# Seventeen loads from the sync queue to the GpSimd queue, unit 0 transposed in full-width tiles, and a new table of order, in a fused attention and feed-forward kernel

## The chip, the cores and the metric

The kernel runs on one core of a Trainium2 chip. The metric is device time in microseconds (us), as the median of several runs. Five engines work side by side, each through its own list of instructions in order: TensorE (PE, matrix products and transposes through PSUM), VectorE (DVE), ScalarE (ACT), GpSimd (POOL) and SyncE (SP, which only issues transfers). Transfers (DMAs) run on 16 DMA engines that all issuers share. An engine that waits for a semaphore holds everything behind it in its list.

## The reference

q, k and v have the shape (batch 8, heads 8, sequence 576, head size 64).

```python
def phi(x):
    proj = np.einsum('bhsd,df->bhsf', x, w_phi)             # 64 -> 128 features
    proj = proj - np.max(np.abs(proj), axis=-1, keepdims=True)
    return np.concatenate([np.exp(proj), np.exp(-proj)], axis=-1)
q_p, k_p = phi(q), phi(k)
kv  = np.einsum('bhsf,bhsd->bhfd', k_p, v);  z = np.sum(k_p, axis=2)
att = np.einsum('bhsf,bhfd->bhsd', q_p, kv) / (np.einsum('bhsf,bhf->bhs', q_p, z)[..., None] + 1e-06)
x   = att.transpose(0, 2, 1, 3).reshape(4608, 512)
out = np.maximum(np.maximum(x @ w1, x @ w2), x @ w3) @ w_out   # 512 -> 768 -> 512
```

## The kernel before, in words

**Attention.** There are 16 units of four heads (half a batch each), u0 to u15. A unit's q, k and v come as 128 partitions x 18 tiles of 64 numbers in f32 (576 KB each). q and k are brought to bf16 and turned so that the head size lies on the partitions (tile `qkT`). How this is done differs by unit. For u0 the loads come in halves through SP (line 441), DVE and ACT cast them (L445), and PE transposes (L483). For u1 to u3 the load itself casts; it is issued by POOL (L452), and PE transposes. From u4 on SP loads f32 (L463), POOL casts (L469), and a transposing DMA on SP's queue does the turn (L498). v is always loaded in f32 through SP (L463). In the units that PE transposes, each 128 x 64 block is one half-width transpose, q and k into different halves of the result, and `qk_bf` is laid out as [q or k, tile, 64].

Then PE projects q and k on the features (L525 and L520, tiles `psq`, `psk`), DVE takes the largest magnitude over the features (L544, results `mqp` for q and `mk` for k), ACT takes both exponentials of k (L538, tile `Ek`), and POOL multiplies v by the factors exp(+-mk) (L579, tile `vab`; line 589 adds the column that gives z). For u0 this multiplication may also be placed on DVE (`VA_DVE`, L49 and L582 ff.). The maximum of q is brought in by a second product (L604, or L606 and L609 for u0 and u1; tile `psm`), and ACT takes its exponentials (L617, tile `Eq`). PE forms kv (L633, 72 small products a unit, called K below), then the numerator and denominator (L651, four groups of ten small products a unit, called N; tile `psn`). DVE divides (L657, L658, tile `x_sb`), and x is turned into `xT` by PE (L671, u0 to u3) or by a transposing DMA (L681).

**Feed-forward.** max(max(a, b), c) @ w_out is computed with w2 and w3 replaced by their differences from w1 (L775: six subtractions of a third of a matrix each, called wd), with relu(x(w2-w1)) (L704 `up`, L712/L714), the maximum with x(w3-w1) (L704, L710) and then two parts of the output: hT @ w_out (L737) and x @ (w1 w_out) (L732). The product w1 w_out is formed once: PE transposes w1 (L787, tile `pwT`), ACT and DVE copy it out (L790), PE multiplies (L801). The weights are loaded with a cast by POOL (L413): W0 is w1, W1 and W2 are the other two, W3 is w_out. There are nine chunks of 512 tokens; the last one holds the 64 leftover rows of each batch.

**What sets the order.** No scheduler runs: every piece of work is a node with a number, and a table in the source (`PLAN`) names for each node its engine (T for PE, D for DVE, A for ACT, G for POOL, S for SP), its buffer numbers and a due time. `1081G@5.1` is node 1081 (the load W0) on POOL, due at 5.1. Instructions are emitted in the order of due times (`fill`, L264), so the table fixes each engine's list; the due times are the planner's and bind nothing on the chip. `fill` also puts idle products (L832, `idler`, one 512-column product each) into gaps of PE's due times in the first 28 us. A node's `costs` lists the engines that may take it.

A POOL or SP load whose buffer is not free waits in its queue for the last reader of that buffer. For v of u1 to u3 a one-element copy on DVE (`gate`, L461) is a further condition for the load.

Of the kernel before, what the change touches and what calls it, by code (L numbers as in the profile page):

```python
# [48 lines left out]
VA_DVE = 1  # L49
# [50 lines left out]
56A@14.3 35D@13.4 50A0@14.8 65A@15.0 104T111211@13.5 66T5@13.8 158G2@3.4 68A@15.5 108D@14.0 30D@14.6 46A@15.8 88T6@14.1  # L100
89D@15.2 92T7@14.9 93D@15.8 107D@16.0 60T3@15.3 61A@16.1 94T46@16.0 98D@16.6 105A@16.6 67A@17.1 99T71@16.8 102D@17.2
96A@17.4 62A@17.9 97D@17.9 101A@18.4 157G@4.2 163T5@17.6 164D2@18.5 1081G@5.1 1091T7@18.1 1092D0@19.1 109T34@18.7 112D@20.2
161T0@19.0 1084G@5.9 106A@18.9 110A@19.4 95A@19.9 1095T5@19.6 1096A@20.3 114T2@20.0 117D@20.8 116A@21.3 103D@21.2 162D@21.8
111A@21.7 1093T7@20.4 52G0@15.2 47G@16.3 115A@22.1 53G@17.4 49G@17.7 51G@18.0 48G@19.1 69T063@21.0 71A@22.5 133T51@22.1
134A@22.9 70A@23.4 130T0@22.6 159D2@22.4 113D@22.5 118D@23.1 1094D@23.5 100A@23.8 135A@24.3 230G0@20.2 1082G@21.0 229G@21.8
74T30@23.0 75D0@24.6 1083G@22.7 119A1@24.8 122G1@25.1 132A@25.0 78T4@23.4 127T2@23.7 136T6@24.1 137A@25.5 72T1@24.6
73D1@25.2 79D0@25.8 182T007500@25.0 185D@26.5 184A@26.0 138A@26.5 123A@26.9 186D@27.1 1099T3@25.4 1100D@27.7 1101T1@26.7
1102D@28.3 131A@27.2 129A@27.7 177T46@28.1 87S@7.4 120G@25.4 121G@26.5 172T70@28.3 175D@28.9 76T3@28.6 183A@28.2 128A@28.7
165T5@28.9 166D@29.5 178A@29.1 173A@29.6 179A@30.1 139T1@29.1 174A@30.6 1103T2@29.3 140A@31.1 1104A@31.4 180D@29.7 77D1@30.3
181D@31.0 187T7@30.6 191D@31.6 126G@27.7 125G@27.9 124G@29.1 142T154@30.9 176D@31.9 144A@32.1 141A@32.5 143A@32.9 367S1@17.2  # L110
370G1@30.2 167T36@31.9 171D@32.5 195A0@33.3 169A@33.5 189A@34.0 198A0@34.4 188A@34.5 1085G@31.3 235T2@32.3 236D0@33.1
170D@33.7 82T0@32.9 80T4@33.1 81A@34.9 145T11@33.4 146D0@34.3 147T5@33.8 148D1@35.0 190D@35.6 1097T2@34.1 168A@35.5 83A@36.0
1098A@36.6 149T3@35.4 150D0@35.9 151T1@35.7 152D1@36.5 233T4@36.0 234D@37.2 254T115711@36.6 256A@37.1 237T6@37.0 238D@37.8
257D@38.0 153T3@37.1 192T0@37.4 193A0@37.7 231D3@38.6 154A@37.9 155T2@37.5 156A@38.6 255A@39.2 160S@22.6 197G@33.7
244T14@37.9 247D@38.7 196G@35.8 214T006@38.2 216A@39.7 215D@39.4 245A@40.1 249T35@39.2 250A@40.6 252D@39.8 239T21@39.5
242D@40.4 240A@41.1 251A@41.6 258D@41.0 1090D@41.6 241A@42.1 1107T0@39.9 366S1@27.2 259T6@40.8 263D@42.2 1087G@37.9
1115T3@41.0 1116A1@42.5 1108A@43.0 261A@43.5 246A@43.9 1109T2@41.9 253D@42.5 369G@40.0 1088D@43.1 1117T7@42.7 1118A@44.4
302S0@32.6 305G2@41.1 194S@38.1 199T30@43.6 211T5@43.8 212A@44.9 213A@45.4 200A@45.7 243D@43.8 262D@44.4 248D@44.7
1129T0@43.9 1130D@45.3 1086G@42.2 1111T1@44.8 208T7@45.6 1112D@45.9 1110D@46.5 209A@46.2 267A1@46.7 264T4@45.9 265A1@46.9
1127T5@45.9 1128D@47.1 1113T0@46.8 202T1@47.7 432S1@38.8 435G0@44.3 232S@39.4 268G1@47.1 260A@47.2 210A@47.5 201A@48.0  # L120
1114A@48.5 205T2@47.9 207A@49.0 371S1@41.2 203A@49.5 204A@50.1 1089D@47.8 206A@50.6 372T004600@48.2 376D@48.6 387T57@48.4
389A@51.1 390D@49.2 375D@49.8 1119T3@48.7 1120D@50.4 301S0@44.1 1125T0@49.6 1126D@51.1 373A@51.6 270G@49.2 1121T5@50.5
388A@52.1 377T41@51.4 380D@51.9 1122D@52.5 382T32@51.7 385D@53.1 374A@52.5 1123T0@52.0 1124D@53.7 378A@53.0 1135T4@52.8
219T60@53.7 392T5@54.0 384A@53.5 379A@54.0 394A@54.5 266S@47.3 368S1@48.0 277T31@54.2 278A@54.8 692S0@48.6 431S1@49.3
283T0@54.5 285A@55.3 383A@55.7 304G@49.6 562S1@49.9 306S2@50.8 561S0@55.9 393A@56.2 284A@56.5 1136T@54.6 1137A0@56.8
1138S@57.6 220D0@54.3 381D@54.9 391D@55.5 386D@56.3 217T6@55.9 218D1@56.9 274T1@56.2 275A@57.4 395D@57.5 396D@58.0 276A@58.1
400A0@58.6 279A@58.8 1131T7@56.4 221T0@57.3 222D0@58.4 269G@50.7 286T124@57.7 288D@59.0 280T6@58.8 281A@59.3 223T5@59.0
397T1@59.3 398D0@59.6 287D@59.8 271T0@59.4 273A@59.8 282A@60.3 272A@60.8 402G0@59.0 434G@61.1 564G1@62.2 565G@63.3
225T3@59.6 226D@60.2 224D1@60.6 1132T@59.9 1133A1@61.4 312T114111@61.3 315D@61.7 307T23@61.5 322T65@61.8 323A@62.2 325D@62.3
293T01@62.1 294D0@62.9 310D@63.6 314A@62.7 324A@63.2 313A@63.7 316D@64.3 1139T7@62.4 326D@64.9 227T4@63.3 228D@65.5  # L130
399S@59.9 404T60@63.5 406A@64.1 309A@64.6 405A@65.1 1140T@63.8 327T0@65.1 328A@65.6 563S0@60.6 407T2@65.3 410T1@65.5
412A@65.9 1141A2@66.4 409A@67.0 311D@66.0 330D@66.6 295T5@65.7 411A@67.5 408A@68.0 331D@67.1 296D1@67.4 291T6@66.0
292D0@68.0 1143T4@66.3 289T7@67.2 290D1@68.6 436S0@62.3 303S2@65.2 496S1@65.8 329A@68.5 498S3@66.5 1144T@67.5 1145D3@69.3
308A@68.8 416T1@68.8 418A@69.3 413T5@68.9 415A@69.7 299T2@69.1 300A@70.2 297T6@69.4 298D@69.9 417A@70.8 317T07@69.8
320D@70.4 321D@71.0 695G2@64.4 403G@65.5 401G@65.8 419T034@70.0 421D@71.6 499G0@71.6 332T6@71.2 333D1@72.0 334S@72.3
335A1@71.7 338G1@72.7 337G@73.0 420D@72.2 1155T2@71.2 1167T0@72.1 1156D0@72.6 1168D@73.3 319A@72.0 414A@72.5 318A@73.0
447T001400@73.1 449A@73.5 452T63@73.3 455D@73.9 453A@74.0 437T52@73.5 439A@74.5 448A@75.0 438A@75.5 454A@75.9 440D@74.5
450D@75.1 441D@76.1 1157T7@73.9 1158A@76.4 1165T0@74.7 457T6@75.6 459A@76.9 428T50@75.8 429D0@76.7 566S1@73.0 628S1@75.9
451D@77.3 461D@77.9 1153T1@76.1 1154A@77.3 1166D@78.3 1149T2@77.0 442T75@77.9 443A@78.4 445D@78.9 1150A@78.9 458A@79.4
444A@79.7 336G@75.1 354T114@78.2 356A@80.2 355D@79.5 424T0@79.3 348T21@79.6 349A@80.6 460D@79.9 425D1@80.2 350A@81.2  # L140
# [145 lines left out]
def kernel(  # L286
# [574 lines left out]
```

## Time and profile before

| | |
|---|---|
| runs | 290.39, 292.25 and 293.01 us; median 292.25 |
| span of the profiled execution | 290.5 us, first to last instruction; 1.75 us below the median |
| PE busy | 276.3 us (95%), 3518 products in the records |
| DVE, ACT, POOL busy | 213.8, 193.8, 116.9 us |
| idle products | 23, 8.6 us of PE |
| loads on SP's queue | 16 of v, 12 of k, 12 of q (576 KB each), 4 halves for u0 |
| transfers issued by POOL | 10 (six q or k with a cast, four weights) |

"Busy" counts the time in which an instruction is in the engine. For PE the products overlap, so its busy time also covers products that follow each other at half the pace; the column PEclk gives the clock that PE was granted (1.00 is full). A wait stands with the instruction that it held, and names what released it.

### The profile page before, as it was taken

How to read it: one execution, taken by the hardware profiler on the slowest of the kernel's cores; microseconds unless marked ns; L12 is line 12 of the kernel's file. 1: busy time of each engine (PE TensorE's matmuls, PEld its weight loads, DVE VectorE, ACT ScalarE, POOL GpSimd, SP SyncE). 2: the span in 40 equal slices, each digit the busy share in tenths (PEclk: the TensorE clock that was granted, in tenths of full speed). 3: DMA queues.
4: the chain of work that ended last, by engine and by line, in shares of the span. 5: the costliest groups of instructions: out<-in, count | busy, mean ns of one | idle time of the engine just before them, and what ended most of it. 6: DMA issues, size and time to landing. Idle time of an engine off the chain costs nothing.

```text
span 290.5 us, 8509 instructions
## 1 busy us (share of the span) xinstructions
PE 276.3 (95%) x3518; PEld 157.4 (54%) x3555; DVE 213.8 (74%) x449; ACT 193.8 (67%) x446; POOL 116.9 (40%) x99
## 2 busy tenths in 40 slices
PE   8678999899999999999999999999999999999995
PEld 3447676356656655555555566555544654444443
DVE  5695899998998967988979879878963382455411
ACT  1795989789898989976797898858758510021021
POOL 8055789728373662817180753500077001000000
PEclk9997999999999999999999999999999999999999
DMA  7999967899999999997999545982240109414045
GB/s 184 280 242 199 246 198 181 197 360 212 231 241 361 150 257 253 275 262 157 225 324 273 118 83 156 164 167 45 52 115 2 39 10 208 91 39 95 12 122 170
DMA packets 65649, 50.83 MB, mean 175 GB/s; under 512 B 46154, under 2 KB 50378, under 8 KB 65610
## 3 DMA queue, kind: packets, MB, share of 16 engines
q1 hardware_dynamic: 61279, 45.03, 63.2%
q0 software_dynamic: 4000, 4.92, 9.9%
q8 instruction: 28, 0.46, 0.6%
q10 hardware_dynamic: 331, 0.33, 0.3%
q14 instruction: 11, 0.09, 0.1%
HBM read 34.67 MB, written 9.44 MB: 152 GB/s over the span
## 4 chain that ended last, share of the span: by engine, by line
PE 66%; DMA 13%; DVE 10%; POOL 5%; issue 2%; SPq 2%; ACT 2%; ACTq 0%; POOLq 0%; DVEq 0%
PE ups L704 22%; PE ops L737 13%; PE ops L732 9%; DMA w_bf<-in_moe_w_dram 6%; PE psn L651 5%; DMA qkT<-qk_bf 5%; PE kvps L633 5%; PE psm L604 3%; PE psq L525 3%; DVE mk L544 3%; DVE hT L710 2%; POOL vab L579 2%; DMA q_raw<-in_q_dram 2%; DVE mqp L544 2%; PE pm L801 2%
## 5 line engine op out<-in xcount | busy, mean ns | idle before, releaser
L704 PE MATMUL ups<-xT,w_bf 128*128 128x512 bf16 x412 | 101.7, 379 | 2.5 <-DVE mk L544 0.9
L617 ACT ACTIVATE Eq<-psm 128x512 bf16<-128x512 f32 (+1 forms) x160 | 82.3, 584 | 9.6 <-PE psm L604 8.2
L579 POOL TENSOR_TENSOR vab<-v_raw,em 128x1152 bf16<-128x1152 f32 (+1 forms) x36 | 67.9, 1904 | 44.6 <-ACT em L575 31.7
L538 ACT ACTIVATE Ek<-psk 128x512 bf16<-128x512 f32 x128 | 70.6, 616 | 8.3 <-PE psk L525 5.1
L704 PEld LDWEIGHTS <-w_bf 128*128 128x128 bf16 x432 | 40.6, 98 | 47.2 <-issue 2.3
L544 DVE TENSOR_REDUCE mqp<-psq 128x4 bf16<-128x512 f32 (+1 forms) x80 | 48.8, 632 | 8.3 <-PE psk L525 4.9
L737 PE MATMUL ops<-wout_bf,hT 128*128 128x512 bf16 (+1 forms) x215 | 50.4, 373 | 0.4
L710 DVE TENSOR_TENSOR hT<-hT,ups 128x512 bf16<-128x512 bf16 x54 | 35.9, 681 | 12.3 <-PE ups L704 8.5
L544 DVE TENSOR_REDUCE mk<-psk 128x4 f32<-128x512 f32 x64 | 42.6, 682 | 1.8 <-PE psk L525 1.1
L745 ACT COPY osb<-ops 128x512 f32<-128x512 f32 (+1 forms) x18 | 10.5, 590 | 38.2 <-PE ops L737 35.7
L737 PEld LDWEIGHTS <-hT 128*128 128x128 bf16 x222 | 21.0, 98 | 22.3
L658 DVE TENSOR_TENSOR x_sb<-psn,rden 128x320 bf16<-128x320 f32 x64 | 31.5, 491 | 2.2
L712 ACT ACTIVATE hT<-ups 128x512 bf16<-128x512 f32 x32 | 19.8, 627 | 17.2 <-PE ups L704 17.2
L651 PEld LDWEIGHTS <-Eq 128*128 128x128 bf16 x640 | 25.2, 97 | 7.7
L651 PE MATMUL psn<-kv_sb,Eq 128*128 128x65 bf16 x640 | 27.3, 194 | 0.0
L745 DVE COPY osb<-ops 128x512 f32<-128x512 f32 (+1 forms) x19 | 12.8, 673 | 19.5 <-PE ops L737 16.4
L732 PE MATMUL ops<-xT 128*128 128x512 bf16 x89 | 24.0, 380 | 0.4
L525 PE MATMUL psq<-w,qkT 64*128 64x128 bf16 x256 | 21.5, 219 | 0.8 <-DMA qkT<-qk_bf 0.8
L604 PE MATMUL psm<-qkT,wphi_m 128*128 128x512 bf16 (+1 forms) x70 | 22.3, 358 | 0.0
L525 PE MATMUL psk<-w,qkT 64*128 64x128 bf16 x256 | 21.4, 219 | 0.0
L714 DVE TENSOR_SCALAR hT<-ups 128x512 bf16<-128x512 f32 x22 | 14.8, 685 | 8.4 <-PE ups L704 8.4
L633 PE MATMUL kvps<-vab,Ek 64*128 64x65 bf16 x1152 | 20.1, 190 | 0.4 <-POOL vab L579 0.4
(76 smaller groups left out, 266.7 us busy)
## 6 DMA issues: line engine op xcount, KB each, us to landing
v_raw<-in_v_dram SPq DMA_DIRECT2D x16, 576.0 KB, 5.4
out_dram<-osb SPq DMA_DIRECT2D x66, 128.0 KB, 2.4
k_raw<-in_k_dram SPq DMA_DIRECT2D x12, 576.0 KB, 4.5
q_raw<-in_q_dram SPq DMA_DIRECT2D x12, 576.0 KB, 6.0
w_bf<-in_moe_w_dram POOLq DMA_DIRECT2D x3, 768.0 KB, 17.0
qk_bf<-in_q_dram POOLq DMA_DIRECT2D x3, 288.0 KB, 10.9
qk_bf<-in_k_dram POOLq DMA_DIRECT2D x3, 288.0 KB, 10.7
wout_bf<-in_moe_w_out_dram POOLq DMA_DIRECT2D x1, 768.0 KB, 21.0
```

Of the source, the lines that this page charges most:

```text
L525: nc.tensor.matmul(ps()[:, i, :], lhsT=cols[r, :], rhs=w2[r, c, :], start=True, stop=True)
L538: nc.scalar.activation(Ek[s]()[:, tiles_of(t0, n), :], of(1), EXP, scale=1.0 - 2.0 * s)
L544: nc.vector.tensor_reduce((mq, mk)[c]()[:, tiles_of(t0, n)], of(c), AXX, ALU.max, apply_absolute_value=True)
L579: (nc.vector if n_.eng == "DVE" else nc.gpsimd).tensor_tensor(vab()[:, g, t0:t1, 0:D], vb()[:, t0:t1, :], em()[:, g, t0:t1].unsqueeze(2).t ...
L617: nc.scalar.activation(Eqb()[s][:, cols], psm()[:, 0:w], EXP, scale=1.0 - 2.0 * s)
L633: nc.tensor.matmul(kvps[ab]()[:, t // NT, g, :], lhsT=Ek[g]()[r, t, :], rhs=vab()[r, g, t, :], start=(t + g == 0), stop=(t == UT - 1 and g ...
L651: nc.tensor.matmul(psn()[:, c, :], lhsT=Eqb()[g][:, t0:t0 + P], rhs=kv()[:, pr, ab, g, :], start=(g == 0), stop=(g == 1))
L658: nc.vector.tensor_tensor(x_sb()[:, pr, :, ab, :], psn()[:, :, 0:D], rden().to_broadcast([P, 5, D]), ALU.mult)
L704: nc.tensor.matmul(ups(), lhsT=w_bf[i + 1][:, ct, j * P:(j + 1) * P], rhs=tokens_of(ct), start=(ct == 0), stop=(ct == CT - 1))
L710: nc.vector.tensor_tensor(hT()[:, j, :], hT()[:, j, :], ups(), ALU.max)
L732: nc.tensor.matmul(ops_()[:, 0:width], lhsT=tile_of(ct, tt), rhs=line_w[c_i > MOVE][:, ct, cols], start=(ct == 0), stop=False)
L737: nc.tensor.matmul(ops_()[:, 0:width], lhsT=hT()[:, j, tt * P:(tt + 1) * P], rhs=wout_bf[:, j, cols], start=False, stop=(j == JT - 1))
```

## The change

1. In `attention`, a load of q, k or v for u4 and later, and a load of v for any unit, may be issued by POOL (a software queue) as well as by SP. The new table uses this for 17 of the 40: v of u0, u1, u4, u6, u7, u13; q or k of u4 (k), u5 (both), u6 (q), u7 (both), u12 (k), u13 (k), u14 (both), u15 (q). The cost that the planner writes down for a POOL issue is 0.75.
2. u0 stores its bf16 q and k as [tile, q or k, 64], as u4 and later do, and PE transposes 128 x 128 blocks (q and k at once): 18 transposes in place of 36 half-width ones. u1 to u3 stay as they were.
3. The multiplication of v may be placed on DVE in every unit, the extra column too; the table uses DVE for the two multiplications of u15 and for three of the 18 extra columns.
4. Each wd may be on DVE or POOL. Before, three were on each; in the new table POOL has five and DVE one.
5. The table is new throughout. Among its other moves: on PE, pairs of N groups that follow each other directly go from 20 to 11 and pairs of projections from 28 to 22; 23 idle products become 29, four of them just ahead of the turn of x of u1 (L671); W1 is issued by POOL right after v of u1 (due 8.8, before 21.0), then q and k of u3 and v of u4; W2 is issued at 35.7 (22.7); k of u5 goes from 17.2 on SP to 18.3 on POOL. In u0 the second half of q is cast on DVE, ahead of the first reductions, and the first half of k on ACT. PE changes between full and divided array 87 times in place of 90.

```diff
-VA_DVE = 1
...
-    queue_of = {"SP": nc.sync, "ACT": nc.scalar}
+    queue_of = {"SP": nc.sync, "ACT": nc.scalar, "POOL": nc.gpsimd}
...
-        qk = buf("qk_bf", QK, [P, 2, UT, D] if by_pe else [P, UT, 2 * D], BF16)
+        qk = buf("qk_bf", QK, [P, 2, UT, D] if by_pe and u else [P, UT, 2 * D], BF16)
...
-                            copy_on[n_.eng](qk()[:, what, ts, :], raw()[:, ts, :])
+                            copy_on[n_.eng](qk()[:, ts, what * D:(what + 1) * D], raw()[:, ts, :])
...
-                mains.append(nd("Lv" if what == 2 else "L", {"SP": 0.62}, lambda what=what, raw=raw: nc.sync.dma_start(
-                    by_pairs(raw()), rows_of(what, u, 0, 2)), gates, [raw],
-                    pipe=(EARLY if u == 0 or u == BY_PE and what == 1 else 1.0) * FULL, hold=-3.0, lat=1.7,
-                    packet=PACKET))
+                n_ = nd("Lv" if what == 2 else "L", {"SP": 0.62, "POOL": 0.75}, None, gates, [raw],
+                        pipe=(EARLY if u == 0 or u == BY_PE and what == 1 else 1.0) * FULL, hold=-3.0, lat=1.7,
+                        packet=PACKET)
+                n_.fn = lambda n_=n_, what=what, raw=raw: queue_of[n_.eng].dma_start(by_pairs(raw()), rows_of(what, u, 0, 2))
+                mains.append(n_)
...
                     for n, t in enumerate(range(UT)[tiles_of(t0, nb)]):
+                        if u == 0:
+                            nc.tensor.transpose(tps()[:, n, :], qk()[:, t, :], ident)
+                            continue
                         for c in range(2):
                             nc.tensor.transpose(tps()[c * D:(c + 1) * D, n, :], qk()[:, c, t, :], ident)
...
-                costs = {"POOL": 0.14 + 0.1085 * (t1 - t0)}
-                if VA_DVE > u:
-                    costs["DVE"] = 0.11 + 0.105 * (t1 - t0)
+                costs = {"POOL": 0.14 + 0.1085 * (t1 - t0), "DVE": 0.11 + 0.064 * (t1 - t0)}
...
-            n_ = va("vd", {"ACT": 0.15, "POOL": 0.28}, None, [n_em], [em, vab])
+            n_ = va("vd", {"ACT": 0.15, "POOL": 0.28, "DVE": 0.15}, None, [n_em], [em, vab])
...
-            n_ = node("wd", 0, {"DVE": 0.6} if i else {"POOL": 2.1}, None, [w_nodes[0], w_nodes[i + 1]], [])
+            n_ = node("wd", 0, {"DVE": 1.2, "POOL": 2.1}, None, [w_nodes[0], w_nodes[i + 1]], [])
...
-0G@0.5 1G@1.2 4A@2.0 2D0@0.8 10S0@0.7 3D@1.1 11D0@4.2 6S0@1.3 7D@5.0 15T1@5.6 5D@5.5 16D0@6.4 86D0@7.2 26T002300@7.2 12S@1.9
+6S0@0.7 0G@0.7 4A@0.7 2D0@0.8 3D@1.0 10S0@1.2 1G@1.3 12S@1.6 84G0@1.9 8S@2.1 85G@2.6 158G1@3.3 14G0@4.0 7D2@4.3
...
```

The table lines themselves (141 before, 147 after) are left out above but for the first of each.

More of the change, by code (lines that the diff above doesn't have):

```diff
@@ L100 @@
[L100 to L104, printed above, removed]
@@ new lines @@
+1156D0@75.1 334S@75.2 450D@75.7 452T24@75.7 1138S@76.0 1149T5@76.0 455D@76.3 336G@76.9 1168D@76.9 1157T6@76.9
+1150A@77.1 1146S@77.2 451D@77.5 439A@77.6 457T2@77.8 424T31@78.0 438A@78.1 1158D@78.1 1153T5@78.3 1134S@78.3 318A@78.5
+460D@78.7 499G1@78.9 456D@79.0 319A@79.0 1165T1@79.2 563S1@79.5 425D0@79.6 453A@79.8 627S1@80.0 498G0@80.0
+354T167@80.1 441D@80.2 1154A@80.3 626S0@80.4 454A@80.7 1105G@80.8 1166D@80.9 442T35@81.2 355A@81.4 356D@81.5
+348T01@81.6 694G@81.7 1169T4@81.8 446D@81.8 350A@82.0 445D@82.4 349A@82.4 587T11111@82.6 422T6@82.8 444A@82.9
@@ new lines @@
+1330D@206.2 1018S2@206.4 1031D@206.8 1361T3@206.8 1356A1@207.0 1322D@207.3 1029A@207.5 989T6@207.7 1349T0@207.9
+1036D@207.9 1066T71@208.8 998T2@208.9 1350D@209.0 1068A@209.1 1054T1@209.1 1323T5@209.3 1067A@209.3 1000A@209.6
+988A@210.1 1347T0@210.2 1038A@210.2 1324D@210.4 1055A@210.7 1353T7@211.0 990A@211.2 1348D@211.2 1056A@211.6
+1362D@211.8 1331T4@211.9 991A@212.1 1354A@212.6 1001T5@212.8 1357T0@212.9 1050A1@213.1 999A@213.3 1051D1@213.4
+1053G@213.5 1351T1@213.7 1063T3@214.6 1052D@214.7 1352A@214.8 1060T6@214.8 1332T@215.0 1064A@215.3 1065A@215.8
@@ L488, in attention @@
                 a = nd("T", {"PE": 0.056 * nb}, tp, [cast[c, j] for c in range(2) for j in need if (c, j) in cast] + [n_ident],
-                       [qk, tps], mode=2)
+                       [qk, tps], mode=2 * (u > 0))
                 c_ = nd("Tc", {"DVE": 0.62 if nb == 8 else 0.22}, None, [a], [tps, qkT], locks=[tps])
```

271 lines of the change are left out of this document (136 added, 135 removed).

## The prediction

> **What bounds the kernel now.** I read the page first, then busy time by stage, then what PE waited for. In the page's second part each digit is a fortieth of the span, 7.26 us.
>
> ```profile
> span 290.5 us, 8509 instructions
> PE 276.3 (95%) x3518; PEld 157.4 (54%) x3555; DVE 213.8 (74%) x449; ACT 193.8 (67%) x446; POOL 116.9 (40%) x99
> ...
> PEclk9997999999999999999999999999999999999999
> ...
> PE 66%; DMA 13%; DVE 10%; POOL 5%; issue 2%; SPq 2%; ACT 2%; ACTq 0%; POOLq 0%; DVEq 0%
> ```
>
> PE holds the end with 66% of the chain, yet one digit of its clock is not a 9. So the stages, from the view of busy time by windows (columns: length; busy time with the number of instructions for PE, weight loads, DVE, ACT, POOL; granted clock; mean load of the DMA engines; GB/s):
>
> ```profile
> 0.00:6.00 6.00, 4.96 (x19) 1.65 (x20) 2.99 (x15) 1.28 (x1) 5.30 (x13) 1.00 0.66 178
> 6.00:12.00 6.00, 3.60 (x66) 2.08 (x61) 2.80 (x7) 2.91 (x6) 0.58 (x1) 1.00 1.10 260
> 12.00:20.00 8.00, 7.74 (x126) 4.67 (x122) 8.00 (x16) 8.00 (x23) 2.28 (x3) 1.00 1.14 266
> 20.00:23.00 3.00, 0.56 (x17) 0.40 (x17) 1.57 (x3) 1.88 (x4) 3.00 (x5) 0.96 1.20 206
> 23.00:26.20 3.20, 3.20 (x40) 2.63 (x41) 1.30 (x2) 1.08 (x2) 2.43 (x4) 0.50 1.19 198
> 26.20:30.00 3.80, 3.80 (x126) 3.26 (x125) 3.32 (x8) 3.46 (x8) 0.00 (x0) 1.00 1.16 195
> 30.00:45.00 15.00, 14.89 (x323) 10.58 (x324) 13.88 (x34) 13.77 (x37) 13.03 (x11) 1.00 0.81 203
> 45.00:60.00 15.00, 13.65 (x147) 6.79 (x142) 14.77 (x23) 13.41 (x33) 13.20 (x9) 1.00 0.91 234
> 60.00:120.00 60.00, 59.05 (x898) 35.60 (x909) 52.35 (x117) 53.94 (x125) 31.87 (x24) 1.00 1.00 258
> 120.00:180.00 60.00, 58.87 (x903) 34.98 (x908) 51.00 (x111) 49.14 (x115) 28.57 (x21) 1.00 0.85 200
> 180.00:240.00 60.00, 59.16 (x679) 32.60 (x687) 42.83 (x93) 38.24 (x88) 15.94 (x12) 1.00 0.41 79
> 240.00:287.00 47.00, 46.79 (x224) 22.09 (x226) 19.00 (x29) 6.30 (x11) 0.74 (x2) 1.00 0.45 103
> ```
>
> From 60 to 287 PE loses 0.95 + 1.13 + 0.84 + 0.21 = 3.1 us of 227; there is hardly a wait to remove. The first 60 us are different. From 12 to 20 DVE and ACT are full (8.00 of 8.00). From 20 to 23 PE is idle for 2.4 us and DVE for 1.4, and then PE is busy but at clock 0.50. From 45 to 60 PE loses 1.35 while DVE is full, and POOL is nearly full from 30 to 60 (26.2 of 30). What PE waited for, and the transfer in the chain of waits (start, length):
>
> ```profile
> PE pwT L787 <- DMA w_bf<-in_moe_w_dram: 2.4, 1, 2.4
> PE tps L483 <- ACT qk_bf L445: 2.4, 1, 2.4
> PE ups L704 <- DVE mk L544: 0.9, 1, 0.9
> ```
> ```profile
> 4.96 17.97 DMA w_bf<-in_moe_w_dram
> ```
> ```profile
> 2.75 5.01 SPq L463 DMA_DIRECT2D v_raw<-in_v_dram  x2
> 7.80 0.47 SPq L463 DMA_DIRECT2D k_raw<-in_k_dram  x1
> 9.60 0.67 ACT L445 CAST qk_bf<-q_raw 128x576 bf16<-128x576 f32 x1 [1.08 <-DMA q_raw<-in_q_dram]
> 10.32 0.69 PE L483 MATMUL tps<-ident,qk_bf 128*64 128x128 bf16 x18 [2.40 <-ACT qk_bf L445]
> 22.98 0.77 PEld L787 LDWEIGHTS <-w_bf 128*128 128x128 bf16 x8 [2.60 <-DMA w_bf<-in_moe_w_dram]
> ```
>
> W0 (w1) lands at 4.96 + 17.97 = 22.93, and PE, which stood before its transposes since 22.98 - 2.60 = 20.38, begins then. Behind it in PE's list stand projections of u1 that DVE and ACT wait for, which is why both are idle too.
>
> **The change part by part.** The rows for the prices (mean ns after the comma):
>
> ```profile
> L579 POOL TENSOR_TENSOR vab<-v_raw,em 128x1152 bf16<-128x1152 f32 (+1 forms) x36 | 67.9, 1904 | 44.6 <-ACT em L575 31.7 <-issue 10.6 <-DMA v_raw<-in_v_dram 2.4
> L544 DVE TENSOR_REDUCE mk<-psk 128x4 f32<-128x512 f32 x64 | 42.6, 682 | 1.8 <-PE psk L525 1.1 <-ACT Ek L538 0.5
> L832 PE MATMUL idler<-idle 128*128 128x512 bf16 x23 | 8.6, 500 | 1.0 <-DVE idle L406 1.0
> L775 POOL TENSOR_TENSOR w_bf<-w_bf 128x1024 bf16<-128x1024 bf16 x3 | 6.8, 2269 | 0.0
> L775 DVE TENSOR_TENSOR w_bf<-w_bf 128x1024 bf16<-128x1024 bf16 x3 | 4.3, 1426 | 0.0
> L452 POOL DMA_DIRECT2D qk_bf<-in_q_dram x3 | 2.4, 803 | 0.0
> L413 POOL DMA_DIRECT2D w_bf<-in_moe_w_dram x3 | 2.4, 787 | 0.0
> L452 POOL DMA_DIRECT2D qk_bf<-in_k_dram x3 | 2.2, 749 | 0.0
> ```
> ```profile
> v_raw<-in_v_dram SPq DMA_DIRECT2D x16, 576.0 KB, 5.4
> ```
> ```profile
> 22.44 0.77 POOL L452 DMA_DIRECT2D qk_bf<-in_k_dram  x1
> ```
>
> *W0.* Until 22.93 the transfers moved 178 x 6 + 260 x 6 + 266 x 8 + 206 x 2.93 = 5360 KB. Ahead of or beside W0 were v of u1 and k of u5, issued by SP by 8.3 (two rows above). Now v of u1 is issued on POOL behind W0 and W3, and k of u5 much later. Two loads of 590 kB less, at 206 to 266 kB a us, are 4.4 to 5.7 us; W0 lands near 18. v of u0 moves to POOL but was ahead of W0 before too. PE comes to W0 at 20.38, so the wait of 2.60 goes. With it goes what I put down to the idle stretch before it: clock 0.50 for 3.2 us, 1.6 us of work. Together 4.2. What is late next is DVE, full until 20: its idle time from 20 to 30 is 10 - 1.57 - 1.30 - 3.32 = 3.8, and more cannot be had. I take **-3.8**; ends 0 (W0 not earlier) and -4.2.
>
> *Opening.* The second half of q is still fourth in SP's queue, so 9.6 stays. The cast moves from ACT (0.67) to DVE, where reductions wait behind it; a reduction (0.68) that had its products before 10.32 now runs after the cast. DVE starts 10.32 - 9.60 = 0.7 earlier with 0.67 + 0.68 more to do, +0.65 at most, and ACT, full from 12 to 20, is spared 0.67: **+0.2**; ends -0.5 and +0.7. The full-width transposes move the same 128 columns once in place of twice half-width at once (18 in 0.69 above), so 0; ends -0.3 and +0.3. Three changes of the array's division fewer are in this.
>
> *wd.* DVE sheds two (2 x 1.43 = 2.9), POOL gains two (2 x 2.27 = 4.5). DVE was full from 45 to 60, where PE lost 1.35, so up to -1.35. But POOL had 26.2 of 30 us from 30 to 60. Adding 4.5, and three issues that now fall there (W2, q of u6, v of u6, 3 x 0.79 = 2.4), less a little, makes about 33 of 30. The products with w3-w1 wait for POOL's wd. I set gain and loss against each other: **0**; ends -1.35 and +3.
>
> *Loads on POOL.* An issue takes (3 x 803 + 3 x 749 + 3 x 787) / 9 = 780 ns of POOL; 17 x 0.78 = 13.3 us, less two multiplications of u15 (4 us), plus wd, makes 131 of 290. After 60 POOL has 76.4 of 180 busy and mostly waits for ACT's factors (31.7), so a load is hidden in those waits: **0**. Without that cover every multiplication behind an issue is 0.78 later, and with it K. No row shows POOL issuing beside a full DVE: the issues lie in 0 to 6 and from 22.44 on (last row above), where DVE is busy about half of the time. The upper bound is one reduction of waiting for each, 17 x 0.68 = 11.6 us of POOL; below zero too, a load that stands no longer behind a transposing DMA in SP's queue can come earlier. I take the row's price, since it is the same instruction; ends -0.4 and +5.8 (half of 11.6 reaching the path).
>
> A rule of the Trainium skill speaks against this term: by SBUF — State Buffer, in the box on DVE blocking a DMA, a transfer issued by GpSimd stalls while DVE runs a two-port copy, since descriptors cannot be written. Its section Who interferes with whom excepts reductions, DVE's largest rows here, so by that rule the term stays near 0, and nothing in this trace can show more.
>
> *Order on PE.* Six more idle products. Two stand ahead of the first transpose and four before the turn of x of u1, where the new list has PE wait for DVE. At full clock one takes about 0.22 (8.6 us over 23 includes the slow start), so 1.3 if all were on the path; they lie in waits: 0, ends 0 and +1.3. Small products that follow each other less often leave DVE and ACT more even work, but from 60 on only 3.1 us can be won: 0; ends -1.5 and +3, as new waits may be drawn.
>
> Sum: -3.8 + 0.2 = -3.6. The profiled execution would have 290.5 - 3.6 = 286.9, and the median 292.25 - 3.6 = **288.6**.
>
> **The rivals.**
>
> *POOL paces u1 to u5 and stays late (slower).* Place: POOL's list from 30 to 60, then each K. It speaks for it that 33 us of work do not fit into 30, against it that some of it (casts for later units) is not urgent. Price: +3 for the overfull stretch, +5.8 if each issue waits for a DVE instruction, with the W0 gain kept: 288.6 + 3 + 5.8 = 297.4. It decides once POOL is busy 15 of 15 in both windows from 30 to 60 and PE waits there for `vab` or `w_bf`.
>
> *The gain is given back to late loads (within 1%).* POOL's queue is one line: v of u4, not needed for a long time, goes ahead of k and q of u5, and W1, q and k of u3 come earlier too. The DMA engines are full until 30 (1.10 to 1.20). 590 kB at 206 to 266 is 2.2 to 2.9 us; if the casts of u5 wait for that, POOL stands with wd and `vab` behind them. 288.6 + 2.6 = 291.2.
>
> *W0 is not earlier.* If the queues share by turns, and casts and v of u0 in one line slow W0: -3.8 becomes 0, 292.4.
>
> *More goes than I count.* DVE's relief from 45 to 60 comes in full (-1.35) and the later waits of PE halve (-1.5): 285.8.
>
> **How the numbers follow.** Likeliest 0.46, POOL paces 0.20, given back 0.18, W0 not earlier 0.04, more gain 0.12. The likeliest one's own range is 286.5 (wd at -1.35 and the opening at -0.5) to 290.3 (the W0 term at -2.1). One per cent, about what a measurement of this kernel can tell from no change, is 2.9 us: faster is below 289.3. Seven tenths of the likeliest and the last case lie there: 0.32 + 0.12 = 0.44. Slower is the first rival, 0.20. The rest, 0.14 + 0.18 + 0.04, is 0.36. The range from 285.0 to 296.0 leaves out half of POOL's case and a third of the last, some 0.14.
>
> **What would show it.** Right: no wait of the L787 transposes for `w_bf`, PEclk without the low digit, DVE idle under 1 us from 20 to 30; PE's loss from 45 to 60 no larger than 1.35; L463 on POOL at 0.75 to 0.8 us; PE losing about 3 us after 60. Wrong: POOL full from 30 to 60 with PE waiting for `vab` or L775; casts L469 waiting for k or q of u5; issues on POOL well above 0.8 us; or a clock of 0.50 elsewhere, since the first 12 us now also hold a wait of over 2 us (the row at 10.32), and there the clock did not fall.

## The result and the profile after

Measured: 304.06 us median (303.65 to 307.04, 4 runs) against 291.96 of the kernel before: ratio 1.043, 95% interval 1.037 to 1.049. The change makes the kernel 4% slower; forecast were 288.6 us. The profiled execution took 303.65 us, its span is 301.7. Ratios and medians below leave out single executions that lie over 1.5% above the fastest of their kernel (296.01 us in e1, 292.57 in e11, 293.45 and 296.54 in e14; the expectations' 290.3 for e1 and 288.8 for e11 have them in).

Line numbers after the change: the extra column of v (called vd below) is L596, wd L782, the turn of x L678, K L640, the transposes of u0 L489, the weight loads L418, the loads of f32 q, k, v L471, POOL's casts L475. In experiments whose table is wrapped anew all are 23 lower. Each wd piece is a third of a matrix; W2 is the load of w3. The page of after:

```profile
span 301.7 us, 8527 instructions
...
PEclk9799995899999999999999999999999999999999
...
PE 79%; DVE 12%; DMA 4%; ACT 3%; issue 1%; SPq 0%
```

Two places of the clock are low now: the second digit (a 7) and the seventh and eighth (5 and 8, from 45 to 60). DVE's share of the chain rose from 10 to 12%, and transfers all but left it (13 to 4%). Busy time by windows, and PE's waits:

```profile
12.00:20.00 8.00, 8.00 (x142) 5.46 (x141) 7.61 (x14) 6.56 (x19) 3.74 (x5) 0.83 1.18 221
20.00:23.00 3.00, 2.81 (x46) 2.04 (x43) 3.00 (x7) 3.00 (x9) 2.67 (x4) 1.00 1.16 295
23.00:26.20 3.20, 3.10 (x98) 2.36 (x97) 3.19 (x9) 3.19 (x9) 1.28 (x2) 1.00 1.15 224
30.00:45.00 15.00, 11.99 (x246) 8.13 (x244) 14.36 (x25) 11.30 (x28) 13.65 (x11) 1.00 0.86 243
45.00:60.00 15.00, 7.83 (x124) 4.86 (x125) 13.69 (x15) 5.52 (x12) 9.97 (x7) 0.66 0.62 155
```
```profile
PE pxT L678 <- DVE x_sb L665: 10.2, 1, 10.2
PE kvps L640 <- DVE vab L596: 3.3, 1, 3.3
PE tps L489 <- DVE qk_bf L450: 2.0, 1, 2.0
```

From 20 to 26.2 PE works at full clock where it had been idle and then at half: that part came as forecast, and no wait for w1 is listed. But from 30 to 60 PE is idle for 10.2 us (3.01 + 7.17) where it had lost 1.5, and PE waits for `x_sb` of DVE, which looks busy (13.69 of 15). The row that holds the loss is a single DVE instruction; beside it what POOL did (start, length), and the same thing once more, smaller, at 73:

```profile
39.84 11.65 DVE L782 TENSOR_TENSOR w_bf<-w_bf 128x1024 bf16<-128x1024 bf16 x1
```
```profile
38.52 0.80 POOL L418 DMA_DIRECT2D w_bf<-in_moe_w_dram  x1
39.32 1.16 POOL L475 CAST qk_bf<-k_raw 128x1152 bf16<-128x1152 f32 x1
40.41 1.15 POOL L475 CAST qk_bf<-q_raw 128x1152 bf16<-128x1152 f32 x1
41.52 2.12 POOL L588 TENSOR_TENSOR vab<-v_raw,em 128x1152 bf16<-128x1152 f32 x1
43.60 2.10 POOL L782 TENSOR_TENSOR w_bf<-w_bf 128x1024 bf16<-128x1024 bf16 x1
45.66 1.13 POOL L475 CAST qk_bf<-k_raw 128x1152 bf16<-128x1152 f32 x1
46.76 4.18 POOL L782 TENSOR_TENSOR w_bf<-w_bf 128x1024 bf16<-128x1024 bf16 x2
```
```profile
73.78 4.02 DVE L596 CAST vab<-em 128x36 bf16<-128x36 f32 x1
```
```profile
73.61 0.75 POOL L471 DMA_DIRECT2D v_raw<-in_v_dram  x1
74.37 1.16 POOL L475 CAST qk_bf<-k_raw 128x1152 bf16<-128x1152 f32 x1
75.46 1.15 POOL L475 CAST qk_bf<-q_raw 128x1152 bf16<-128x1152 f32 x1
76.55 1.15 POOL L475 CAST qk_bf<-k_raw 128x1152 bf16<-128x1152 f32 x1
```

Both DVE instructions end just after POOL's last one of an unbroken run: 39.84 + 11.65 = 51.49 against 46.76 + 4.18 = 50.94, and 77.80 against 77.70. Busy is not working here. The 3.3 us at `kvps` are PE's wait for the second of the two, the extra column of u3. The theory (A): DVE's instruction with two operands in SBUF, or a cast within SBUF, shares something with POOL and is shut out while POOL runs on. The rivals: (B) the piece waited for its data or another engine; (C) the 17 loads on POOL, or the new order as such, are slow.

### The profile page after: what moved, and what is told of

It reads as the page before. It is cut to its first block, busy times and chain, and to the rows that moved or that the text cites. A ratio compares the mean times of both kernels' runs of the same rounds, so it can differ in the third digit from the quotient of the medians.

```text
span 301.7 us, 8527 instructions
## 1 busy us (share of the span) xinstructions
PE 279.7 (93%) x3543; PEld 157.7 (52%) x3543; DVE 226.8 (75%) x443; ACT 194.2 (64%) x450; POOL 129.8 (43%) x118
## 4 chain that ended last, share of the span: by engine, by line
PE 79%; DVE 12%; DMA 4%; ACT 3%; issue 1%; SPq 0%
PE ups L711 30%; PE ops L744 14%; PE ops L739 10%; PE psn L658 6%; PE kvps L640 5%; PE psm L611 5%; PE psq L534 5%; DVE w_bf L782 4%; DMA q_raw<-in_q_dram 2%; DMA qkT<-mT 2%; DVE mqp L553 2%; DVE vab L596 2%; DVE mk L553 1%; ACT Eq L624 1%; PE psq L529 1%; PE pm L808 1%
## 5 line engine op out<-in xcount | busy, mean ns | idle before, releaser
L711 PE MATMUL ups<-xT,w_bf 128*128 128x512 bf16 x432 | 103.5, 380 | 0.0
L588 POOL TENSOR_TENSOR vab<-v_raw,em 128x1152 bf16<-128x1152 f32 (+1 forms) x34 | 63.8, 1891 | 71.4 <-ACT em L584 45.2
L624 ACT ACTIVATE Eq<-psm 128x512 bf16<-128x512 f32 (+1 forms) x160 | 80.2, 582 | 8.6 <-PE psm L611 6.2
L752 ACT COPY osb<-ops 128x512 f32<-128x512 f32 (+1 forms) x22 | 12.9, 593 | 36.5 <-PE ops L744 34.0
L658 PEld LDWEIGHTS <-Eq 128*128 128x128 bf16 x640 | 26.4, 97 | 9.3
L719 ACT ACTIVATE hT<-ups 128x512 bf16<-128x512 f32 x30 | 18.3, 620 | 19.7 <-PE ups L711 19.7
L658 PE MATMUL psn<-kv_sb,Eq 128*128 128x65 bf16 x640 | 28.5, 194 | 0.0
L721 DVE TENSOR_SCALAR hT<-ups 128x512 bf16<-128x512 f32 x24 | 16.5, 687 | 12.5 <-PE ups L711 12.3
L752 DVE COPY osb<-ops 128x512 f32<-128x512 f32 (+1 forms) x15 | 10.1, 671 | 20.3 <-PE ops L744 15.7
L640 PE MATMUL kvps<-vab,Ek 64*128 64x65 bf16 x1152 | 20.0, 190 | 3.3 <-DVE vab L596 3.3
L534 PE MATMUL psq<-w,qkT 64*128 64x128 bf16 x256 | 22.7, 223 | 0.0
## 6 DMA issues: line engine op xcount, KB each, us to landing
w_bf<-in_moe_w_dram POOLq DMA_DIRECT2D x3, 768.0 KB, 13.7
```

What stands on the lines that cost most here:

```text
L534: nc.tensor.matmul(ps()[:, i, :], lhsT=cols[r, :], rhs=w2[r, c, :], start=True, stop=True)
L588: (nc.vector if n_.eng == "DVE" else nc.gpsimd).tensor_tensor(vab()[:, g, t0:t1, 0:D], vb()[:, t0:t1, :], em()[:, g, t0:t1].unsqueeze(2).t ...
L624: nc.scalar.activation(Eqb()[s][:, cols], psm()[:, 0:w], EXP, scale=1.0 - 2.0 * s)
L640: nc.tensor.matmul(kvps[ab]()[:, t // NT, g, :], lhsT=Ek[g]()[r, t, :], rhs=vab()[r, g, t, :], start=(t + g == 0), stop=(t == UT - 1 and g ...
L658: nc.tensor.matmul(psn()[:, c, :], lhsT=Eqb()[g][:, t0:t0 + P], rhs=kv()[:, pr, ab, g, :], start=(g == 0), stop=(g == 1))
L711: nc.tensor.matmul(ups(), lhsT=w_bf[i + 1][:, ct, j * P:(j + 1) * P], rhs=tokens_of(ct), start=(ct == 0), stop=(ct == CT - 1))
```

## The experiments

**e1, the piece on POOL.** One table entry of the changed kernel.

```diff
-1087D@37.0
+1087G@37.0
```

> The changed kernel (304.1 us) with one entry of its table altered: the third piece of w2 - w1 (wd, L782), which took DVE 11.65 us at 39.84 while POOL ran seven instructions without a break, goes to POOL at the same place. Theory A (DVE's instruction with two operands in SBUF is kept out while POOL runs back to back): the piece takes POOL about 2.1 us, PE's wait of 10.4 us for x_sb at 52 and the half clock after it are gone, the time falls by 10 to 14 us to 290-294. What stays is the wait of 3.4 us at 78 (vd of u3 on DVE). Rival B (the piece waited for its data or for another engine): POOL now waits for the same, the wait moves along, 300-304. Rival C (the loads that POOL issues, or the order itself, make the kernel slow): 300-304.

Measured: 290.24 us, ratio to before 0.988 (0.980 to 0.996). B and C fall: POOL runs the piece at 40.25 in 2.13 us without a wait, and 13.8 of the 304.06 us hang on this one entry. The wait of 3.3 us at 78 went too, since vd of u3 came at another moment, when POOL stood still (0.24 us at 63.32).

**e2, one operand in place of two.**

```diff
-                (nc.vector if n_.eng == "DVE" else nc.gpsimd).tensor_tensor(dst[:, :, c], dst[:, :, c], w_bf[0][:, :, c],
-                                                                           ALU.subtract)
+                if n_.eng == "DVE":
+                    nc.vector.tensor_reduce(dst[:, :, c].rearrange("p a (n o) -> p a n o", o=1),
+                                            dst[:, :, c].rearrange("p a (n o) -> p a n o", o=1), AXX, ALU.max)
+                    return
...
```

> The changed kernel with the DVE instruction of that piece replaced by one of the same shape at the same place, with the same waits, that reads one operand instead of two (a maximum over a single element, which copies; one third of w2 - w1 is left out). Theory A: it takes 1 to 1.6 us beside the same POOL instructions, and the time is 288-292. Rival B (its data or another engine are late): it lasts or waits until 51 as before, 300-304.

```profile
38.04 1.21 DVE L783 TENSOR_REDUCE w_bf<-w_bf 128x1024 bf16<-128x1024 bf16 x1
```

Same place, same waits, same POOL run beside it: 1.21 us in place of 11.65. One execution, 287.50 us (span 285.6); a third of w2-w1 is left out of it. So the form of DVE's instruction matters. That it is the second operand alone is not shown: the cast at 73.78 reads one operand, and it was shut out too.

**e3, my term for W0 alone.** The changed code with the table of before and two entries of it altered.

```diff
-87S@7.4
...
-367S1@17.2
+87G@8.1
...
+367G1@18.3
```

> The changed code with the table of before, save that two loads, v of u1 and k of u5, are issued by POOL behind W3 instead of by SP: my term for W0 by itself, with u0's full-width transposes. If the term holds (w1 lands some 2 us earlier, PE's wait of 2.6 us before L794 shrinks and the half clock after it goes), 287.5-289.5. If those two loads were not what held w1 up, or the wait only moves, 291.5-293.

Measured: 293.44 us, ratio 1.004 (1.000 to 1.008): no gain. W0 landed 13.7 us after its issue at 4.96, so the wait for it was gone, but PE then waited for another transfer, q of u3, 3.6 us, followed by half clock (0.50 from 37 to 41):

```profile
PE tps L486 <- DMA qk_bf<-in_q_dram: 3.6, 1, 3.6
```

With the old table this load is issued at 23.03 and takes 13.99 us to land; the new table issues it at 12.5.

**e4 and e5, the collision by itself.** POOL runs of casts, products and subtractions, and one DVE instruction set off with them (shortened):

```python
nc.gpsimd.memset(go, 1.0)                            # lets DVE go
for f in ops: f()                                    # POOL's run, no waits
nc.vector.tensor_reduce(done, go, AXX, ALU.max)      # DVE waits for go
on_dve()                                             # subtraction, cast or maximum
nc.vector.memset(go, 0.0)
```

> None of the kernel's work is in it: streaks of POOL instructions without waits (eight casts, four subtractions, four products, a mix), each let go together with one DVE instruction: a subtraction of 4 x 256 with two operands in SBUF, a cast of 36 elements, a maximum that reads one operand. Theory A in its strong form (POOL back to back keeps DVE out until it pauses): the subtraction lasts until the end of the whole streak, 8 to 9 us beside eight casts, and the maximum 1 to 1.6 us in every case. Weak form (DVE gets its turn at the first end of a POOL instruction, as in the kernel before): the subtraction lasts 1 to 2.5 us beside any streak, and the 11.65 us have some other cause. A DMA issue between the casts should let DVE in, by what vd of u1 showed (1.17 us).

> None of the kernel's work is in it. The same streaks again, now with the DVE instruction set off at 15 different moments after the streak's first POOL instruction began, in steps of about 0.06 us: the kernel's own order (cast, cast, product, subtraction, cast, two subtractions) and six casts beside a subtraction in place of two operands, and a DMA issue followed by three casts beside a cast of 36 elements. The first probe showed DVE let in at the first end of a POOL instruction in all 14 meetings, so the strong form of theory A fell, and the kernel's six lost turns need a reason. Theory A2 (the moment decides): for some offsets, near the 0.52 us of the kernel, DVE loses one or more turns and lasts 4 to 11 us; for the others 1 to 2.5 us. Theory A3 (something else of the kernel, absent here, takes the turn away): DVE is let in at the first end at every offset, at most 2.8 us.

Groups of e4 (count, total, mean in ns), then of e5:

```profile
L110 DVE TENSOR_TENSOR wa<-wb,wb 128x1024 bf16<-128x1024 bf16 x12 | 19.8, 1648 | 0.0
```
```profile
L116 DVE CAST vd<-es 128x36 bf16<-128x36 f32 x15 | 51.3, 3421 | 0.0
L113 DVE TENSOR_TENSOR w<-w,w 128x1024 bf16<-128x1024 bf16 x30 | 33.3, 1111 | 0.0
```

In plain runs DVE is let in at the first end of a POOL instruction, in every meeting of e4 and at all 30 offsets of e5 (0.68 to 1.73 us): the strong form of A fell, and so did A2, by which the moment decides. The cast in e5 was shut out for all three POOL casts in 14 of 15 meetings; the 15th asked before the DMA issue and took 0.24 us. What sets these apart is the DMA issue at the head of POOL's run (and DVE's cast in place of its subtraction, which e10 takes up). Both long waits of the kernel have one there too: W2 at 38.52, v at 73.61. That is theory A4.

**e6, both kinds of collision avoided.**

```diff
-1087D@37.0
-126D@25.6
-270D@59.6
-858D@187.7
+1087G@31.5
+126A@25.6
+270A@59.6
+858A@187.7
```

> The changed kernel with four entries of its table altered, so that DVE no longer meets POOL in SBUF before the last unit: the wd piece on POOL 5.5 us earlier in the table (behind the piece at 30.8, where POOL stood idle 1.34 us in the run with the piece on POOL), and the three vd copies that the table gave to DVE (u1, u3, u12) on ACT. Theory A: neither the wait of 10.4 us nor the one of 3.4 us at 78 comes, the span is 285-288 and the time 287-290, below the 290.3 of the run with the piece late in POOL's streak. If the loads on POOL or the order cost by themselves, 291 or more.

Measured: 287.69 us, ratio 0.985 (0.981 to 0.990), 1.5% below the kernel before and far below the changed one. Its windows are the change without the collisions:

```profile
30.00:45.00 15.00, 14.70 (x304) 10.04 (x304) 12.97 (x31) 14.22 (x36) 14.99 (x12) 1.00 0.81 230
45.00:60.00 15.00, 14.94 (x172) 7.83 (x165) 13.26 (x25) 14.06 (x34) 14.16 (x10) 1.00 1.11 295
60.00:120.00 60.00, 59.56 (x911) 35.06 (x908) 50.05 (x108) 52.88 (x125) 40.64 (x33) 1.00 0.99 244
120.00:180.00 60.00, 59.25 (x898) 34.41 (x896) 49.68 (x109) 49.38 (x115) 30.91 (x26) 1.00 0.96 207
180.00:240.00 60.00, 60.00 (x683) 32.71 (x682) 42.94 (x88) 35.98 (x84) 9.77 (x5) 1.00 0.36 72
```

**e7, the same with the 17 loads on SP.** In the table of e6 the G of each of the 17 loads becomes S, due times kept.

> The kernel of the run beside it (wd piece early on POOL, vd on ACT) with the 17 loads that the change moved to POOL issued by SP again, at the same places of the table. If the loads on POOL cost nothing and bring nothing (my term: 0, ends -0.4 and +5.8), the same time as its neighbour within 1.5 us, save for v of u1 and k of u5, which would be back beside w1's load: up to 3 us slower. If POOL's queue was paced by its loads, 2 to 5 us faster.

Measured: 294.85 us, ratio to before 1.010 (1.005 to 1.015): 7.2 us slower than e6 beside it. It is all in the opening: PE waits 3.5 us for w1 again, which lands 21.0 us after its issue at 4.96, and then has half clock. From 60 to 180 PE's busy time is that of e6 (59.71 and 59.20). But e7 puts more beside w1 than the kernel before had: SP also issues v of u4 and q of u5 by 8.7 us, and POOL issues W1 at 6.53 (10.15 in e6, 23.20 before). So the 7.2 us are not the worth of v of u1 and k of u5 alone.

```profile
PE pwT L771 <- DMA w_bf<-in_moe_w_dram: 3.5, 1, 3.5
```

**e9, the piece one step later on DVE.** `1087D@37.0` becomes `1087D@38.4`.

> The changed kernel with the wd piece still on DVE, put behind one more of DVE's instructions for x_sb (one step of about 0.6 us later). Theory A2 (the moment at which DVE asks decides): likely let in at the first or second end of a POOL instruction, 1 to 3 us for the piece, the time 287-292. If a streak without a break always keeps DVE out in this kernel: the piece lasts until POOL stops near 51, the wait moves to the next user of x_sb, 299-304.

306.32 us (one execution): the piece asked 1.21 us after the casts began in place of 0.52 and still lasted 10.96 us. A2 fell in the kernel as well. But POOL made no pause here: DVE lost five turns and got in at the end of the subtractions (50.46), while POOL went straight on with a cast, which took 1.60 us in place of 1.13:

```profile
40.04 10.96 DVE L759 TENSOR_TENSOR w_bf<-w_bf 128x1024 bf16<-128x1024 bf16 x1
```
```profile
50.41 1.60 POOL L452 CAST qk_bf<-q_raw 128x1152 bf16<-128x1152 f32 x1
```

**e10, the DMA issue varied.**

> None of the kernel's work is in it. In the phase probe DVE was let in at the first end of a POOL instruction in all 30 meetings with plain streaks, and in none of 14 where a DMA issue by POOL stood at the streak's head (it waited 3.2 to 4.1 us, for all three casts). Theory A4: it is the DMA issue ahead, in an unbroken streak, that keeps DVE out until POOL pauses. Then beside a DMA issue and ten casts DVE's subtraction lasts 11 to 12.5 us, beside a DMA issue and four subtractions or products 9 to 10 us; with the DMA issue in the middle of the casts it is let in at the first end if it asks before the DMA issue (0.6 to 1.8 us) and shut out to the end if it asks after it (5 us or more); a pause of POOL on another engine ends it (under 2 us where it asks after the pause). Rival A3: it was the length of the cast on DVE or the short streak, and the subtraction beside ten casts takes under 3 us. A maximum that reads one operand, and a subtraction that reads its second operand from PSUM, take about 1.2 and 0.5 us throughout.

Rows of the second pass through the list (the first gave the same within 0.1 us where DVE asked at the same point):

```profile
127.25 12.06 DVE L125 TENSOR_TENSOR w<-w,w 128x1024 bf16<-128x1024 bf16 x1
151.47 3.28 DVE L125 TENSOR_TENSOR w<-w,w 128x1024 bf16<-128x1024 bf16 x1
161.26 9.47 DVE L125 TENSOR_TENSOR w<-w,w 128x1024 bf16<-128x1024 bf16 x1
178.36 1.21 DVE L147 TENSOR_REDUCE vd<-slow 128x1 bf16<-128x1024 bf16 x1
185.71 0.41 DVE L144 TENSOR_TENSOR w<-w,ps 128x256 bf16<-128x256 bf16 x1
193.02 8.79 DVE L125 TENSOR_TENSOR w<-w,w 128x1024 bf16<-128x1024 bf16 x1
237.53 0.98 DVE L125 TENSOR_TENSOR w<-w,w 128x1024 bf16<-128x1024 bf16 x1
```

In this order: beside a DMA issue and ten casts 12.06 us, shut out to the end; with four subtractions 3.28, let in at the first end; with four products 9.47, shut out; the maximum and the subtraction with its second operand in PSUM are untouched. (The latter is a quarter as long and was over at 186.12, while POOL was still issuing the DMA, so it met no cast.) A DMA issue of 512 bytes shut DVE out as well (7.53 us in the first pass). The moment of asking mattered as expected: just before a DMA issue in the middle of the casts DVE took 0.68 us (214.00); 0.39 us after one at the head of six casts it took 6.74, to their end (222.47). Two rows do not fit A4. At 193.02 DVE asked before the DMA issue of its own run, but POOL had come without a break from a run that began with one; it lost seven turns and then got the eighth. At 237.53 it asked during a DMA issue and was let in at about that issue's end. With e9, where no pause ended the wait, that is three. So a DMA issue ahead is what the shut-outs have in common, but it does not settle every meeting, and POOL's subtractions, which the trace shows 0.08 us apart in the probe, let DVE in.

**e11 and e12, A4 in the kernel, both ways.** In e11 W2 is issued 2.1 us earlier in the changed kernel's table; the piece stays on DVE. In e12 the kernel before gets one tiny load more.

```diff
-1083G@35.7
+1083G@33.6
```
```diff
...
+            def to_qk(c=c):
+                if (u, c) == (4, 1):
+                    nc.gpsimd.dma_start(extra, w_phi[0:1, 0:DF])
+                nc.gpsimd.tensor_copy(qk()[:, :, c * D:(c + 1) * D], raw_bufs(u)[c]())
...
```

> The changed kernel with one entry of its table moved: the load of w3, which POOL issues directly ahead of its seven instructions at 39, goes 2.1 us earlier, into POOL's idle time ahead of a product of u2. The wd piece stays on DVE at its place, beside the same streak. Theory A4 (the DMA issue at the head of the streak shuts DVE out): the piece lasts 0.7 to 2.6 us, the wait of 10.4 us is gone, 288-292 (the 3.4 us of vd u3 stay, or go if the phases move). Theory A in its strong form (the streak alone shuts it out): 10 us or more as before, 302-306.

> The kernel before with one instruction more: POOL issues a load of 512 bytes that nobody reads, directly ahead of the cast that ran at 47.23, beside which DVE's wd took 0.96 us at 47.96. Theory A4: that wd now lasts until POOL pauses at about 53, 4 to 5 us, the work of u3 and u4 behind it is late, and the time rises by 2 to 5 us to 294-297. Rival (a DMA issue is only its own 0.75 us of POOL): 292-293, the wd pieces 1 to 2.6 us.

e11: 287.60 us, ratio 0.986 (0.980 to 0.993), the piece 1.48 us. e12: 296.04 us, ratio 1.014 (1.009 to 1.018); a load of 512 bytes cost 4.2 us, since the piece that had taken 0.96 now took 4.73, shut out from a cast, a subtraction and a cast, and PE waited 3.3 us for the `mk` behind it. DVE and POOL before, then in e12:

```profile
47.96 0.96 DVE L775 TENSOR_TENSOR w_bf<-w_bf 128x1024 bf16<-128x1024 bf16 x1
49.77 1.68 DVE L775 TENSOR_TENSOR w_bf<-w_bf 128x1024 bf16<-128x1024 bf16 x1
55.29 1.63 DVE L775 TENSOR_TENSOR w_bf<-w_bf 128x1024 bf16<-128x1024 bf16 x1
```
```profile
47.23 1.15 POOL L469 CAST qk_bf<-k_raw 128x1152 bf16<-128x1152 f32 x1
48.34 2.57 POOL L775 TENSOR_TENSOR w_bf<-w_bf 128x1024 bf16<-128x1024 bf16 x1
```
```profile
46.89 4.73 DVE L779 TENSOR_TENSOR w_bf<-w_bf 128x1024 bf16<-128x1024 bf16 x1
```
```profile
46.19 0.57 POOL L472 DMA_DIRECT2D extra<-in_w_phi_dram  x1
```

The turn that DVE gets is taken from POOL: before, POOL's subtraction at 48.34, beside which DVE was let in, took 2.57 us; the one at 44.08, with none of DVE's three beside it, took 2.12.

**e13 and e14, the pause.** e13 is e11 with the three vd copies on ACT (the last three edits of e6); e14 is e13 with vd of u1 on DVE again.

> The run beside it (w3's load moved, wd piece on DVE) with the three vd copies of DVE (u1, u3, u12) on ACT. Theory A4: the wd piece lasts 0.7 to 2.6 us and no vd is shut out, so that the span is 284.5-288 and the time 286-290, like the 287.7 of the kernel with the piece on POOL or up to 2 us under it, since POOL's streak is 2.1 us shorter.

> The kernel that took 301.9 us with w3's load moved and three vd copies on ACT, with one of the three, vd of u1, on DVE again. In the 288.8 us kernel (all three on DVE) POOL paused 0.61 us between the load of w3 and its run of instructions, in the 301.9 us kernel 0.02 us. Theory A4 with the pause deciding: if vd of u1 on DVE (1.16 us of DVE at 27) is what delays ACT's factors of u2, the pause of about 0.6 us is back, the wd piece lasts 0.7 to 1.7 us and the time is 286-290. If POOL goes straight on behind the load, the piece is shut out for over 10 us, 299-303. A piece shut out for over 10 us in spite of a pause of 0.5 us, or let in without any pause, would fell the theory.

e13: 301.92 us, ratio 1.033 (1.027 to 1.039), a miss: the piece lasted 14.16 us, the longest of all. e14: 288.02 us from two executions (the profiled one has a span of 286.0); the other two took 293.45 and 296.54, and no trace shows why. The piece took 1.48 us in the profiled one. POOL and the piece in e13, then in e14:

```profile
34.25 0.79 POOL L395 DMA_DIRECT2D w_bf<-in_moe_w_dram  x1
35.07 2.14 POOL L565 TENSOR_TENSOR vab<-v_raw,em 128x1152 bf16<-128x1152 f32 x1
```
```profile
38.30 14.16 DVE L759 TENSOR_TENSOR w_bf<-w_bf 128x1024 bf16<-128x1024 bf16 x1
```
```profile
34.40 0.80 POOL L395 DMA_DIRECT2D w_bf<-in_moe_w_dram  x1
35.80 2.11 POOL L565 TENSOR_TENSOR vab<-v_raw,em 128x1152 bf16<-128x1152 f32 x1 [0.60 <-ACT em L561]
```
```profile
39.16 1.48 DVE L759 TENSOR_TENSOR w_bf<-w_bf 128x1024 bf16<-128x1024 bf16 x1
```

With vd of u1 off DVE, ACT's factors come sooner and POOL goes straight on from the load of w3 (0.02 us between). With it, POOL waits 0.60 us, and DVE, which asks 3.4 us after that pause, gets in at the first end. With the pause of 0.6 us behind the DMA issue the piece takes 1.48 us, without it 14.16.

**e15, how long a pause.**

> None of the kernel's work is in it. POOL: a DMA issue, a cast, then a wait for ACT that is drawn out in 24 steps of about 0.045 us from nothing to about 1 us, then six casts; DVE asks with its subtraction of two operands well behind the wait, within the six casts. Theory A4: without a pause DVE is shut out to the end of the casts (4 to 5 us); from some length of pause on it is let in at the first end (0.7 to 1.8 us). The length at which it turns over says how much of a pause POOL needs: between 0.02 us (not enough in the kernel) and 0.6 us (enough).

Inconclusive on the length: ACT was done early, so that POOL never paused. Still DVE took 1.26 to 1.47 us in the 23 meetings with an unbroken run: the wait was carried by a copy of 128 x 8, and after that short POOL instruction DVE was let in without any pause. For the same reason the like rows of e10 prove nothing on pauses. Not every short instruction does this: behind the 128 x 8 memset at 192.82 in e10 DVE, asking at 193.02, was shut out.

## Why the prediction was wrong

*wd* is the step that failed. I set it at 0 with ends of -1.35 and +3, by weighing two pieces off DVE (2 x 1.43) against two more on POOL (2 x 2.27). The one entry that left a piece on DVE cost 13.8 us (304.06 - 290.24), through a collision that the balance of busy times cannot show: 10.2 us of PE's wait for `x_sb` with a clock of 0.66 from 45 to 60, and 3.3 us behind vd of u3, which went with the same entry. Without the collision the balance itself fell on the good side of my 0: from 30 to 60 PE loses 0.36 us in e6, with all six pieces on POOL, and lost 1.46 before. The row that I priced it by held the sign: a mean of 1426 ns over three pieces of 0.96, 1.68 and 1.63 us at 47.96, 49.77 and 55.29, where the same subtraction took 0.68 when POOL stood still (e12, at 52.48). Each had ended 0.54 to 0.55 us after the POOL instruction then running. I read a price where there was a wait.

*Loads on POOL.* As a cost of POOL's time, 0 was right: e7 and e6 agree from 60 on, and an issue took the 0.75 to 0.8 us of the rows. But DMA issues make POOL's runs shut DVE out. The DMA issue ahead of the 3.3 us before K of u3 is one of the 17 (v, at 73.61). I looked for the harm in the other direction, by the box of the Trainium skill's page SBUF — State Buffer on DVE blocking a transfer. That page's section Who interferes with whom also says that a DVE instruction with two SBUF inputs contends with a GpSimd instruction that reads SBUF, and that a cast on DVE can; both moves were in the change, and I left the sentence out. The traces agree on which instructions are affected (1.21 us for a reduction, 11.65 for a subtraction with two operands in SBUF, 4.02 in place of 0.24 for the cast); the subtraction with one operand in PSUM (0.41) fits, but it met a DMA issue only. The section has the port held for one whole instruction; it does not tell of turns lost one after another, and there the measurement decides.

*W0* was right in mechanism and nearly in size. It landed at 5.67 + 13.7 = 19.4 us (I had said near 18), 4.3 us sooner after its issue than before, and PE's wait and the half clock behind it are gone. In e7, where that is undone, 7.2 us are lost, more than my 4.2, since w1 then lands at 26.0, behind loads that the kernel before did not issue so early. What I gave as the second rival, the gain handed on to a late load, is what e3 shows with the old table.

*Opening*: +0.2 was too kind. The wait of 2.0 us for q is followed by a clock of 0.83 from 12 to 20, some 1.4 us of work. I had named this as a way to be wrong. What brings the clock down there stays open; the length of the wait does not settle it. With waits of 2.6 and 1.3 us e6 and e11 have 0.85 and 0.82, with 1.5 and 1.1 us e1 and e2 have full clock, and the kernel before had it with 2.4.

*Order on PE*: set at 0, ends -1.5 and +3; e6 loses 0.44 + 0.75 + 0.00 = 1.2 us from 60 to 240, all of it in two waits for `qkT`. Before lost 2.9 there, but its list of waits names only 1.4 of them (0.8 for `qkT`, 0.4 for `vab`, 0.2 for `hT`), and its records hold 3518 products beside 3555 weight loads (3543 and 3543 after), so the rest can be products that are missing from the records. The order was worth between 0.2 and 1.7 us there, and the 3.1 us that I read as lost are an upper bound. *Transposes of u0* as said: nine full-width ones take 0.66 us where 18 half-width ones took 0.69.

The first rival, POOL pacing u1 to u5, fell: in e6 POOL is as full as I feared (14.99 and 14.16 of 15), and PE loses 0.36 us. After the change PE did not wait for POOL's results but for DVE's, behind two instructions. Without the collisions the sum stood: forecast 286.9 for the span, e6 286.9, e11 285.7, e2 285.6. That it fits to the tenth in e6 is partly luck: the clock of 0.85 from 12 to 20 costs 1.2 us that I had not counted, and from 30 to 60 it gains 1.1 us that I had set at nothing.

## What to carry to other kernels

Before placing a DVE instruction with two SBUF operands, or a cast within SBUF, look at what POOL runs beside it: a DVE row much longer than its twin elsewhere that ends just behind a POOL instruction is waiting, not working. Above all keep it away from an unbroken run of POOL work behind a DMA issued by POOL; putting the piece on POOL (e1), moving the DMA issue ahead of an idle moment of POOL (e11) and, for the test, a reduction in its place (e2) each removed more than 13 us here. And test such a collision with the order and idle times of the real kernel, since 0.6 us of idle time decided it (e13 against e14).

## What the runs showed that I had not expected

In plain POOL runs DVE got in at the first end in all 30 offsets (0.68 to 1.73 us); behind a DMA issue it waited through ten casts in e10 (12.06 us) and through eight instructions in e13 (14.16 us), and a DMA issue of 512 bytes was enough (4.73 us in e12). A later DMA issue ended the wait in e13 (the piece ended at 52.46, while POOL issued q from 51.86), but not in e10 at 193.02. In e9 it ended with neither a pause nor a DMA issue. After a 128 x 8 copy on POOL DVE was let in (e15), after a 128 x 8 memset it was not (e10). Why is open. The Trainium skill, Perfetto Trace Analysis, section DMA Instruction — SWDGE (GPSIMD), says that only two of GpSimd's processors write the descriptors; the others might then run ahead, so that no moment is left between two instructions at which all have let go. That was not tested, and the two rows of e10 and the end of the wait in e9, which fall outside A4, would have to follow from it.
